# An MLP's first product on two row tiles: which output tiles share a two-bank PSUM buffer, and where the last eviction stands

## The chip, the cores and the metric

The kernel runs on one core of a Trainium2 chip. The metric is the device time of one execution in microseconds (us), as the median of several runs. The engines of the core run side by side, each through its own queue in order: TensorE (PE in the profile; its weight loads are PEld), VectorE (DVE), ScalarE (ACT), GpSimd (POOL) and SyncE (SP), which only issues transfers here. They wait for each other by semaphores.

## The reference

Four residual layers on a sequence of 2048 tokens with 576 features, in turn linear attention (A) and MLP (B), each applied to the layer-normalised input. The same weights serve both A layers and both B layers.

```python
B, S, D, F = 1, 2048, 576, 4608

def _B_ref(x, w1, b1, w2, b2):
    y = _layernorm(x, axis=-1)
    h = _gelu(jnp.einsum("bsd,df->bsf", y, w1) + b1)
    return jnp.einsum("bsf,fd->bsd", h, w2) + b2

x = x + _A_ref(_layernorm(x, axis=-1), A_wqkv, A_wo)
x = x + _B_ref(_layernorm(x, axis=-1), B_w1, B_b1, B_w2, B_b2)
x = x + _A_ref(_layernorm(x, axis=-1), A_wqkv, A_wo)
x = x + _B_ref(_layernorm(x, axis=-1), B_w1, B_b1, B_w2, B_b2)
```

The change is in the first product of the MLP, `y @ w1`, with its gelu.

## The kernel before

The tokens of an MLP layer are worked on in 4 chunks of 512. For one chunk the first product makes hT, the gelu of 4608 hidden features by 512 tokens, as 36 tiles of 128 x 512; `m1_group` makes four of them (n = 0 to 3), so a chunk has 9 groups, a layer 36, and the kernel 72. Then the second product (L546 to L560) makes four output tiles of 128 tokens from hT and w2, with accumulators of two PSUM banks, and adds the residual.

The contraction has 576 = 4 x 128 + 64 rows. [...] The odd 64 rows (`w1_tail`) go to the upper or the lower row tile by the parity of the tile. So each of the four tiles has nine matmuls, 4 or 5 from each row tile, and a group has 18 upper and 18 lower ones, interleaved one by one into 18 steps (numbered 0 to 17 here). The upper row tile takes the tiles in the order 0, 1, 2, 3, the lower one in the order 2, 3, 0, 1 (L501, L502):

| Steps | Upper row tile | Lower row tile |
|---|---|---|
| 0 to 3 | tile 0 | tile 2 |
| 4 | tile 0 | tile 3 |
| 5 to 8 | tile 1 | tile 3 |
| 9 to 12 | tile 2 | tile 0 |
| 13 | tile 2 | tile 1 |
| 14 to 17 | tile 3 | tile 1 |

Tile 0 is complete at step 12, tile 2 at step 13, tiles 3 and 1 at step 17. The order of TensorE's matmuls in the MLP is fixed by a chain of dependencies (`pe`).

Where a tile passes from one row tile to the other (from step 9 on), the matmul must not overlap the last one of the other row tile on the same bank. This is enforced over ScalarE: a tiny copy (L518, the relay) waits for the last matmul of the first holder, and the first matmul of the second holder waits for the relay. There are two relays in a group: one behind step 4 (tile 0's upper half; it lets tiles 0 and 2 change hands at step 9), one behind step 8 (tile 3's lower half; for tiles 1 and 3 at steps 13 and 14).

The four tiles lie in PSUM as follows: two buffers of one bank from the pool `ps_h`, which rotates over three, and a pair of banks from `ps_acc`, which has two such pairs used in turn (`next_acc`), the accumulators of the second product among them. Line 489 says which tile lies where: tiles 0 and 1 in the h buffers, tiles 2 and 3 in the pair. When a tile is complete, ScalarE evicts it with gelu and bias into hT (L524); ScalarE thus has the relays and the evictions in its queue. Dependencies between engines are found by the framework from the buffers that instructions read and write; a scheduler sets the order of each engine's instructions, as far as the chain and the dependencies leave it open.

The first two groups of a layer's first chunk are emitted in the tail of the attention layer before it (`a2_hook`, which calls `m1_group` after the last steps of that layer), so their matmuls can be placed between that layer's projections (`wo_ps`, L442), transposes (`to_ps`, L432) and numerators (`nd_ps`, L405). The buffer of hT overlays `abig`, the attention layer's buffer that the output projection reads.

Of the kernel before, what the change touches and what calls it, by code (L numbers as in the profile page):

```python
# [7 lines left out]
ACT = mybir.ActivationFunctionType  # L8
# [27 lines left out]
def build(tc, A_x, A_wqkv, A_wo, B_w1, B_b1, B_w2, B_b2, out, dbg=None, n_layers=4):  # L36
    nc = tc.nc
    dbg = dbg or {}
    with ExitStack() as ctx:
# [39 lines left out]
        b1T = const.tile([P, NF], F32, name="b1T")  # L79
# [30 lines left out]
        def pe(inst):  # L110
            if pe_chain["on"]:
                if pe_chain["last"] is not None:
                    tc.add_manual_dep(inst.ins, pe_chain["last"], NOSYNC, reason="TensorE order in the MLP")
                pe_chain["last"] = inst.ins.name
            return inst
# [10 lines left out]
        for t in range(5):  # L126
            load_x0(t)
        chained(nc.sync.dma_start(out=wqkv_sb[:, 0:4, D:3 * D],
                                  in_=A_wqkv[0:4 * P, D:3 * D].rearrange("(k p) n -> p k n", p=P)))
        chained(nc.sync.dma_start(out=wqkv_sb[0:64, 4, D:3 * D], in_=A_wqkv[4 * P:D, D:3 * D]))  # L130
        chained(nc.sync.dma_start(out=wqkv_sb[:, 0:4, 0:D],
                                  in_=A_wqkv[0:4 * P, 0:D].rearrange("(k p) n -> p k n", p=P)))
# [54 lines left out]
        class LNPipe:  # L187
            def __init__(self):
                self.items = []
# [86 lines left out]
        def prefetch_xo(li, t, add_b2):  # L276
            if li == 0:
                xo = work.tile([P, D], BF16, name="xbf", tag="xbf", bufs=5)
                nc.sync.dma_start(out=xo[:], in_=x_in[t * P:(t + 1) * P, :])
            else:  # L280
                xo = work.tile([P, D], F32, name="xo", tag="xo", bufs=3)
                nc.sync.dma_start(out=xo[:], in_=x_d[t])
            if add_b2:
                nc.gpsimd.tensor_tensor(out=xo[:], in0=xo[:], in1=b2_bc[:], op=ALU.add)  # L284
            xo_of[(li, t)] = xo

        def residual(li, t, halves):
            xo = xo_of.pop((li, t))
            last = (li == n_layers - 1)
            if last:  # L290
                xn = work.tile([P, D], BF16, name="xbf", tag="xbf", bufs=5)
            else:
                xn = work.tile([P, D], F32, name="xn", tag="xn", bufs=3)
            nc.vector.tensor_tensor(out=xn[:].rearrange("p (h n) -> p h n", h=2), in0=halves,  # L294
                                    in1=xo[:].rearrange("p (h n) -> p h n", h=2), op=ALU.add)
            if last:
                nc.sync.dma_start(out=out_f[t * P:(t + 1) * P, :], in_=xn[:])
                return None
            nc.sync.dma_start(out=x_d[t], in_=xn[:])
            return xn  # L300
# [165 lines left out]
        def next_acc():  # L466
            acc_turn["n"] += 1
            return ("accA", "accB")[acc_turn["n"] % 2]

        GF = 4  # L470
        NGRP = NF // GF

        class LayerB:
            def __init__(self, li, next_kind):
                self.li = li
                self.next_kind = next_kind
                self.hT = {}
                self.done = {}

            def m1_group(self, c, g):  # L480
                if c not in self.hT:
                    if c == 0:
                        acc_turn["n"] = 1
                    self.hT[c] = big.tile([P, NF, CB], BF16, name="hT", tag="big")
                hT = self.hT[c]
                ctok = slice(c * CB, (c + 1) * CB)
                hps = [ps_h.tile([P, 512], F32, name="h_ps", tag="h") for _ in range(2)]
                pair = ps_acc.tile([P, 2, 512], F32, name="hp_ps", tag=next_acc())
                dst = [hps[0][:], hps[1][:], pair[:, 0, :], pair[:, 1, :]]

                def half_blocks(n, hi):
                    f = g * GF + n
                    rows = slice(64 * hi, 64 * hi + 64)
                    ops = [(n, w1_sb[rows, k, f * P:(f + 1) * P], yT[rows, k, ctok]) for k in range(KD - 1)]
                    if f % 2 == hi:
                        fc = f // 2 * P
                        ops.append((n, w1_tail[rows, fc:fc + P], yT[rows, KD - 1, ctok]))
                    return ops

                was_on, pe_chain["on"] = pe_chain["on"], True  # L500
                upper = [op for n in (0, 1, 2, 3) for op in half_blocks(n, 0)]  # L501
                lower = [op for n in (2, 3, 0, 1) for op in half_blocks(n, 1)]  # L502
                seen = [0] * GF
                order = [(hi, n, wt, mv) for step in zip(upper, lower) for hi, (n, wt, mv) in enumerate(step)]
                first, last = {}, {}
                for i, (hi, n, _, _) in enumerate(order):
                    first.setdefault((hi, n), i)
                    last[(hi, n)] = i
                relay_at = {last[(0, 0)]: (0, 2), last[(1, 3)]: (1, 3)}
                starts = {first[(1, 0)]: 0, first[(0, 2)]: 2, first[(1, 1)]: 1, first[(0, 3)]: 3}  # L510
                relay_of = {}
                for i, (hi, n, wt, mv) in enumerate(order):
                    mm = pe(nc.tensor.matmul(dst[n], lhsT=wt, rhs=mv, start=(seen[n] == 0), stop=(seen[n] == 8)))  # L513
                    seen[n] += 1
                    if i in starts:
                        tc.add_manual_dep(mm.ins, relay_of[starts[i]], SYNC, reason="row tiles take turns on a PSUM bank")
                    if i in relay_at:
                        relay = nc.scalar.copy(out=relay_sb[:, 1:2], in_=relay_sb[:, 0:1])  # L518
                        tc.add_manual_dep(relay.ins, mm.ins.name, SYNC, reason="row tiles take turns on a PSUM bank")
                        for m in relay_at[i]:  # L520
                            relay_of[m] = relay.ins.name
                    if seen[n] == 9:
                        f = g * GF + n
                        nc.scalar.activation(out=hT[:, f, :], in_=dst[n], func=ACT.Gelu_apprx_tanh,  # L524
                                             bias=b1T[:, f:f + 1], scale=1.0)
                pe_chain["on"] = was_on
                self.done[c] = g + 1

            def run(self):
                li, next_kind = self.li, self.next_kind  # L530

                def feed_next(c, i):
                    if c + 1 < NCB:
                        t = (c + 1) * TPC + i
                        lnp.feed(None, t, "B", "dve", "dve", load_from=t)

                for c in range(NCB):
                    for g in range(self.done.get(c, 0), NGRP):
                        self.m1_group(c, g)
                        if g in (3, 5):  # L540
                            prefetch_xo(li, c * TPC + (g - 3) // 2, add_b2=True)
                        if g in (4, 6):
                            feed_next(c, (g - 4) // 2)
                        lnp.tick(transposes=0)
                    hT = self.hT.pop(c)
                    for j in range(TPC):  # L546
                        t = c * TPC + j
                        acc = ps_acc.tile([P, 2, 512], F32, name="m2_ps", tag=next_acc())
                        for f in range(NF):
                            for half in range(2):  # L550
                                pe(nc.tensor.matmul(acc[:, half, 0:HALF], lhsT=hT[:, f, j * P:(j + 1) * P],  # L551
                                                    rhs=w2_sb[:, f, half * HALF:(half + 1) * HALF],
                                                    start=(f == 0), stop=(f == NF - 1)))
                            if f % 12 == 6:
                                if j == 0 and f in (6, 18):
                                    feed_next(c, 2 + f // 18)
                                lnp.tick()
                            if f == 18 and j < 2:
                                prefetch_xo(li, c * TPC + 2 + j, add_b2=True)
                        xn = residual(li, t, acc[:, :, 0:HALF])  # L560
                        if xn is not None and next_kind == "A":
                            lnp.feed(xn, t, "A", "dve", "dve")
# [110 lines left out]
```

## Time and profile before

| | us |
|---|---|
| Median of 3 runs (lowest, highest) | 908.98 (908.51, 909.83) |
| The profiled execution's own time | 908.65 |
| Its span in the trace | 906.6 |
| TensorE busy | 801.6 (88%) |
| ScalarE busy | 356.9 (39%) |
| VectorE busy | 270.4 (30%) |
| GpSimd busy | 106.2 (12%) |
| First product, second chunk of layer 1 (window 214.6 to 261.5) | 46.9, TensorE busy 36.7 |
| Second product behind it (window 261.5 to 299.0) | 37.5, TensorE busy 37.5 |
| Granted TensorE clock from 117 us on | 1.00 (0.96 before) |

A line of the profile names the source line (L513 is line 513), the engine, the operation, the tile written, an arrow, the tiles read, and the shape. Tile names in it are the program's: `h_ps` and `hp_ps` are the h buffers and the pair of the first product, `m_ps` the accumulator of the second, `w_sb` any of the weights. Busy time of TensorE is modelled: its matmuls are pipelined, and the 376 ns that each matmul of L513 has in the profile overlap the next one. Idle time is put down to the instruction whose semaphore event came last before the wait ended. Matmuls and their weight loads are separate instructions; a wait can stand at either.

### The profile page before, as it was taken

What the parts mean: (1) busy time and instruction counts of PE and PEld (TensorE: products, weight loads), DVE (VectorE), ACT (ScalarE), POOL (GpSimd) and SP (SyncE); (2) the same over time, 40 slices, a digit from 0 to 9 for tenths busy, and PEclk for the clock granted to TensorE, in tenths of its full rate; (3) what the DMA queues carried; (4) which work ended last, traced back from release to release, by engine and by line L of the source; (5) the groups of instructions that cost most, each with busy time, mean ns of one, the idle gap of its engine ahead of it and who ended that gap; (6) DMA issues with size and microseconds to landing.
All of it is one profiled execution on the core that took longest, in us unless ns stands there. A gap on an engine that the chain in (4) does not pass through costs nothing.

```text
span 906.6 us, 16729 instructions
## 1 busy us (share of the span) xinstructions
PE 801.6 (88%) x7030; PEld 538.2 (59%) x7030; DVE 270.4 (30%) x850; ACT 356.9 (39%) x746; POOL 106.2 (12%) x199
## 2 busy tenths in 40 slices
PE   5999987798789879978999998879977987898798
PEld 3787654485358436734877776436734854584366
DVE  4757960035014402300244599202300300010001
ACT  4686735402530351055227674551055015303510
POOL 5410300012002201100100011201100210011000
PEclk8899999999999999999999999999999999999999
DMA  8970640012012100100110047201200210020000
GB/s 217 274 242 24 213 164 1 1 53 79 2 27 80 53 1 27 54 27 1 53 54 1 2 153 249 96 1 47 81 5 2 66 40 1 1 57 23 1 21 20
DMA packets 42907, 56.97 MB, mean 63 GB/s; under 512 B 10256, under 2 KB 26896, under 8 KB 42832
## 3 DMA queue, kind: packets, MB, share of 16 engines
q1 hardware_dynamic: 42832, 55.91, 20.3%
q8 instruction: 55, 0.90, 0.4%
q14 instruction: 20, 0.16, 0.1%
HBM read 39.38 MB, written 16.52 MB: 62 GB/s over the span
## 4 chain that ended last, share of the span: by engine, by line
PE 79%; ACT 11%; DVE 4%; issue 2%; DMA 1%; POOL 1%; DVEq 0%; POOLq 0%; ACTq 0%
PE m_ps L551 31%; PE h_ps L513 15%; PE hp_ps L513 15%; ACT hT L524 10%; PE q_ps L351 4%; PE k_ps L319 3%; PE v_ps L330 2%; PE wo_ps L442 2%; PE v_ps L327 2%; PE tp L250 2%; DVE xn L294 1%; PE kvacc L343 1%; PE to_ps L432 1%; DVE o_ring L416 1%; PE nd_ps L405 1%
## 5 line engine op out<-in xcount | busy, mean ns | idle before, releaser
L513 PE MATMUL hp_ps<-yT,w_sb 64*128 64x512 bf16 x1152 | 274.1, 376 | 81.4 <-ACT hT L524 81.4
L551 PE MATMUL m_ps<-w_sb,hT 128*128 128x288 bf16 x2304 | 289.8, 286 | 0.0
L513 PE MATMUL h_ps<-yT,w_sb 64*128 64x512 bf16 x1152 | 286.0, 377 | 0.0
L513 PEld LDWEIGHTS <-w_sb 64*128 64x128 bf16 x2304 | 137.5, 94 | 215.0 <-issue 104.5
L551 PEld LDWEIGHTS <-hT 128*128 128x128 bf16 x2304 | 223.2, 98 | 57.9 <-issue 3.4
L518 ACT COPY relay_sb<-relay_sb 128x1 f32<-128x1 f32 x144 | 27.4, 190 | 272.5 <-PE h_ps L513 224.0
L524 ACT ACTIVATE hT<-hp_ps,b1T 128x512 bf16<-128x512 f32 x144 | 98.4, 683 | 78.7 <-PE h_ps L513 78.7
L524 ACT ACTIVATE hT<-h_ps,b1T 128x512 bf16<-128x512 f32 x144 | 98.4, 683 | 45.0 <-PE h_ps L513 43.3
L254 DVE COPY yT<-tp 128x640 bf16<-128x640 bf16 x40 | 19.6, 490 | 323.5 <-PE tp L250 323.4
L225 POOL TENSOR_TENSOR ln_rstd<-ln_u,neg_half 128x1 f32<-128x1 f32 x64 | 36.0, 563 | 359.5 <-DVE ln_u L218 217.4
L284 POOL TENSOR_TENSOR xo<-xo,b_bc 128x576 f32<-128x576 f32 x32 | 40.8, 1276 | 177.4 <-DMA xo<-x_d 177.3
L513 PE MATMUL h_ps<-yT,w_tail 64*128 64x512 bf16 x144 | 54.1, 376 | 0.0
L513 PE MATMUL hp_ps<-yT,w_tail 64*128 64x512 bf16 x144 | 54.1, 376 | 0.0
L351 PE MATMUL q_ps<-yT,wqkv_sb 128*126 128x512 bf16 (+1 forms) x200 | 51.8, 381 | 0.0
L442 PE MATMUL wo_ps<-wo_sb,abig 128*128 128x288 bf16 x320 | 46.5, 286 | 5.0 <-ACT abig L434 3.4
L270 DVE TENSOR_SCALAR phi_e<-phi_e 128x288 bf16<-128x288 bf16 (+2 forms) x104 | 30.1, 290 | 60.9 <-ACT phi_e L267 60.4
L294 DVE TENSOR_TENSOR xbf<-m_ps,xo 128x576 bf16<-128x576 f32 x16 | 12.1, 758 | 119.2 <-PE m_ps L551 119.2
L319 PE MATMUL k_ps<-wqkv_sb,yT 128*128 128x288 bf16 x320 | 47.0, 294 | 0.0
L243 POOL COPY y_ring<-y_ring 128x64 bf16<-128x64 bf16 x64 | 15.4, 244 | 228.5 <-DVE y_ring L241 199.1
L267 ACT ACTIVATE phi_e<-k_ps 128x288 bf16<-128x288 f32 x64 | 26.8, 420 | 37.3 <-PE k_ps L319 33.9
L442 PEld LDWEIGHTS <-abig 128*128 128x128 bf16 x320 | 29.4, 98 | 15.8 <-ACT abig L434 6.0
L272 DVE TENSOR_TENSOR abig<-phi_a,phi_e 128x288 bf16<-128x288 bf16 (+2 forms) x104 | 36.1, 348 | 7.6 <-ACT phi_a L269 1.8
(78 smaller groups left out, 696.4 us busy)
## 6 DMA issues: line engine op xcount, KB each, us to landing
x_d<-xn SPq DMA_DIRECT2D x48, 288.0 KB, 2.2
xo<-x_d SPq DMA_DIRECT2D x48, 288.0 KB, 3.0
xl<-x_d SPq DMA_DIRECT2D x24, 288.0 KB, 3.0
w_sb<-in_B_w_dram SPq DMA_DIRECT2D x6, 864.0 KB, 11.1
xbf<-in_A_x_dram SPq DMA_DIRECT2D x32, 144.0 KB, 3.4
w_sb<-in_B_w_dram SPq DMA_DIRECT2D x9, 512.0 KB, 5.0
out_dram<-xbf SPq DMA_DIRECT2D x16, 144.0 KB, 1.7
wqkv_sb<-in_A_wqkv_dram SPq DMA_DIRECT2D x1, 1152.0 KB, 7.8
```

The lines of the kernel that those rows point to most:

```text
L225: nc.gpsimd.tensor_tensor(out=rstd[:], in0=it["u"][:], in1=neg_half[:], op=ALU.pow)
L267: nc.scalar.activation(out=e[0:rows, 0:n], in_=ps_ap, func=ACT.Exp)
L270: nc.vector.tensor_scalar(out=e[0:rows, 0:n], in0=e[0:rows, 0:n], scalar1=1.0, scalar2=1e-6, op0=ALU.min, op1=ALU.add)
L272: nc.vector.tensor_tensor(out=out_ap, in0=a[0:rows, 0:n], in1=e[0:rows, 0:n], op=ALU.max)
L284: nc.gpsimd.tensor_tensor(out=xo[:], in0=xo[:], in1=b2_bc[:], op=ALU.add)
L319: nc.tensor.matmul(kp[:, 0:HALF], lhsT=yT[:, k, tok], rhs=wqkv_sb[:, k, D + half * HALF: D + (half + 1) * HALF], start=(k == 0), stop=(k = ...
L351: nc.tensor.matmul(qp[0:GR[g], :], lhsT=wqkv_sb[:, k, GO[g]:GO[g] + GR[g]], rhs=yT[:, k, c * CA:(c + 1) * CA], start=(k == 0), stop=(k == ...
L442: nc.tensor.matmul(wp[:, half, 0:HALF], lhsT=oT[:, k, :], rhs=wo_sb[:, k, half * HALF:(half + 1) * HALF], start=(k == 0), stop=(k == KD - 1))
L513: mm = pe(nc.tensor.matmul(dst[n], lhsT=wt, rhs=mv, start=(seen[n] == 0), stop=(seen[n] == 8)))
L518: relay = nc.scalar.copy(out=relay_sb[:, 1:2], in_=relay_sb[:, 0:1])
L524: nc.scalar.activation(out=hT[:, f, :], in_=dst[n], func=ACT.Gelu_apprx_tanh, bias=b1T[:, f:f + 1], scale=1.0)
L551: pe(nc.tensor.matmul(acc[:, half, 0:HALF], lhsT=hT[:, f, j * P:(j + 1) * P], rhs=w2_sb[:, f, half * HALF:(half + 1) * HALF], start=(f == ...
```

## The change

Tiles 1 and 2 change places: tiles 0 and 2 lie in the h buffers now, tiles 1 and 3 in the pair. Tile 3's eviction is no longer emitted where the tile is complete, but held: it is emitted behind the next group's first relay, or, for a chunk's last group, ahead of the second product (`flush`). The matmuls, their order in the MLP, the number of relays and of evictions, and the buffers' sizes stay.

```diff
+                self.held = None
...
-                dst = [hps[0][:], hps[1][:], pair[:, 0, :], pair[:, 1, :]]
+                dst = [hps[0][:], pair[:, 0, :], hps[1][:], pair[:, 1, :]]
...
+                def evict(n):
+                    f = g * GF + n
+                    nc.scalar.activation(out=hT[:, f, :], in_=dst[n], func=ACT.Gelu_apprx_tanh,
+                                         bias=b1T[:, f:f + 1], scale=1.0)
+
                 for i, (hi, n, wt, mv) in enumerate(order):
...
                         for m in relay_at[i]:
                             relay_of[m] = relay.ins.name
-                    if seen[n] == 9:
-                        f = g * GF + n
-                        nc.scalar.activation(out=hT[:, f, :], in_=dst[n], func=ACT.Gelu_apprx_tanh,
-                                             bias=b1T[:, f:f + 1], scale=1.0)
+                        if i == last[(0, 0)]:
+                            self.flush()
+                    if seen[n] == 9 and n != 3:
+                        evict(n)
+                self.held = lambda: evict(3)
...
+            def flush(self):
+                if self.held is not None:
+                    self.held()
+                    self.held = None
...
                         lnp.tick(transposes=0)
+                    self.flush()
                     hT = self.hT.pop(c)
```

## The prediction

> **What bounds the kernel now.** I first read the page's chain of the work that ended last, for the engine to look at.
>
> ```profile
> PE 79%; ACT 11%; DVE 4%; issue 2%; DMA 1%; POOL 1%; DVEq 0%; POOLq 0%; ACTq 0%
> PE m_ps L551 31%; PE h_ps L513 15%; PE hp_ps L513 15%; ACT hT L524 10%; PE q_ps L351 4%; PE k_ps L319 3%; PE v_ps L330 2%; PE wo_ps L442 2%; PE v_ps L327 2%; PE tp L250 2%; DVE xn L294 1%; PE kvacc L343 1%; PE to_ps L432 1%; DVE o_ring L416 1%; PE nd_ps L405 1%
> ```
>
> TensorE sets the time, except that a tenth of the chain is the gelu eviction of L524. So I asked the view of waits who waits for that.
>
> ```profile
> ACT hT L524 <- PE h_ps L513: 122.0, 141, 1.1
> PE hp_ps L513 <- ACT hT L524: 81.4, 72, 1.4
> ```
>
> The columns are total us, times, and the longest. There are 2 MLP layers x 4 chunks x 9 groups = 72 groups, so TensorE waits once in each. The timeline of one group shows where (start, duration; in brackets the idle time and who ended it).
>
> ```profile
> 148.79 0.38 PE L513 MATMUL h_ps<-yT,w_sb 64*128 64x512 bf16 x1
> 148.99 0.38 PE L513 MATMUL hp_ps<-yT,w_tail 64*128 64x512 bf16 x1
> 149.20 0.69 ACT L524 ACTIVATE hT<-h_ps,b1T 128x512 bf16<-128x512 f32 x1 [0.62 <-PE h_ps L513]
> 149.79 0.68 ACT L524 ACTIVATE hT<-hp_ps,b1T 128x512 bf16<-128x512 f32 x1
> 150.52 0.37 PE L513 MATMUL hp_ps<-yT,w_sb 64*128 64x512 bf16 x1 [1.14 <-ACT hT L524]
> 151.38 0.38 PE L513 MATMUL h_ps<-yT,w_sb 64*128 64x512 bf16 x1
> 151.58 0.69 ACT L524 ACTIVATE hT<-hp_ps,b1T 128x512 bf16<-128x512 f32 x1 [1.11 <-PE h_ps L513]
> 152.16 0.68 ACT L524 ACTIVATE hT<-h_ps,b1T 128x512 bf16<-128x512 f32 x1
> 152.73 0.19 ACT L518 COPY relay_sb<-relay_sb 128x1 f32<-128x1 f32 x1
> 153.59 0.19 ACT L518 COPY relay_sb<-relay_sb 128x1 f32<-128x1 f32 x1 [0.67 <-PE hp_ps L513]
> 154.19 0.38 PE L513 MATMUL hp_ps<-yT,w_tail 64*128 64x512 bf16 x1
> 154.40 0.69 ACT L524 ACTIVATE hT<-h_ps,b1T 128x512 bf16<-128x512 f32 x1 [0.62 <-PE h_ps L513]
> ```
>
> A group has 18 steps (0 to 17), each one matmul of the upper and one of the lower row tile; the row at 148.79 is step 12 (tile 0's last), 148.99 step 13 (tile 2's last), 150.52 step 14 (tile 3's first upper), 151.38 step 0 of the next group. Step 14 writes one bank of the pair buffer, and starts 0.05 us after the eviction of tile 2, which reads the other bank (149.79 + 0.68 = 150.47): TensorE waits for a reader of the same buffer, not of the same data. Nothing else stops it: from 150.52 (step 14) to 154.19 (step 13 of the next group) 17 steps take 3.67 us, 0.216 each, so 18 need 3.89, and the group takes 154.40 - 149.20 = 5.20. The wait costs 1.31 a group (the row's 1.14 plus pipelining lost).
>
> **What the change removes.** Tiles 1 and 3, which end together at step 17, now share the pair; tiles 0 and 2 have an h buffer each. The write of step 14 then meets no pending reader. Of 72 groups, 70 wait like this one; the first group of each MLP layer is taken below. 70 x 1.31 = 92.0 us removed, if nothing takes its place.
>
> **What may take its place.** The h buffers rotate over three slots, two a group, so tile 2 of the next group needs the slot from which tile 0 was evicted. Set T at step 0 of the next group. Tile 0's last matmul (step 12, lower) starts at T - 6 x 0.216 + 0.02 = T - 1.28; its eviction starts 0.41 later (148.79 to 149.20) and lasts 0.69, and TensorE answers within 0.05: T - 0.13. The first lower matmul stands at T + 0.02: hidden by 0.15 us, cover thin enough to name. If it were gone, each 0.1 us of lateness costs 64 x 0.1 = 6.4 us (8 groups with a predecessor in each of 8 chunks).
>
> ScalarE's queue: evictions follow each other at 0.585 (149.20 to 149.79), a relay copy 0.57 behind an eviction (152.16 to 152.73). Tile 0 at T - 0.87, tile 2 at T - 0.28, tile 1 at T + 0.30, tile 3 at T + 0.89. The title says that the fourth eviction stands behind the next group's first relay copy. In the built program's order it does not: in the steady groups ScalarE has tiles 0, 2, 1, 3 and then both relay copies, as the scheduler puts what is ready first. So what is queued behind the held eviction is the relay copy, at T + 1.46 to 1.65, where it was 1.35 to 1.54 after step 0. Its reader is step 9, matmul at T + 1.94, weight load some 0.2 earlier: still in time, by about 0.1. The second relay waits for step 8 (T + 1.74 + 0.46 = T + 2.20, ends 2.39; needed at step 13, T + 2.82), and tile 0's next eviction is due at T + 3.02. Price of both places: I take 0; the far end, one more eviction pitch in the way, would be 0.585 - 0.15 = 0.43 us a group, 64 x 0.43 = 28 us. The held closure adds no instruction; the flush before the second product keeps tile 3's eviction ahead of its reader (f = 35, some 70 matmuls of L551 at 0.1225 = 8 us later): 0.
>
> ScalarE as the bound: 4 x 0.683 + 2 x 0.190 = 3.11 us busy a group against TensorE's 3.89; no. [...]
>
> **The two joints from attention to MLP.** There the first eviction waits for the last output projection, since the MLP's hT overlays the buffer that this reads:
>
> ```profile
> 131.47 1.28 ACT L524 ACT_TABLE_LOAD   x1
> 132.17 1.40 PE L442 MATMUL wo_ps<-wo_sb,abig 128*128 128x288 bf16 x10
> 133.61 0.69 ACT L524 ACTIVATE hT<-h_ps,b1T 128x512 bf16<-128x512 f32 x1 [0.86 <-PE wo_ps L442]
> 134.93 0.37 PE L513 MATMUL hp_ps<-yT,w_sb 64*128 64x512 bf16 x1 [1.35 <-ACT hT L524]
> ```
>
> Before, group 1 starts at 135.78, 2.21 after the projection's end at 133.57. In the changed order the table load also stands behind that end, and group 0 is complete ahead of it; group 1's first lower matmul waits for 0.04 + 1.28 + 0.69 + 0.05 = 2.06 us. Gain 2 x 0.17 = 0.3. [...] The four steps that group 0 no longer has behind the projection (4 x 0.216 = 0.86) must fit into TensorE's gaps ahead of it, where it waits 0.38 to 0.84 us at a time; and VectorE now normalises (L241, 0.57) ahead of a residual and an o_ring. Bounds: 0 to 2 x (0.86 + 0.76) = 3.2; I take 1.0, since the timeline from 117 to 129 us shows TensorE idle 0.38, 0.84, 0.84 and 0.77 us there, room for the 0.86 at least.
>
> **MLP to attention, layer 1 to 2.** Seven k_ps matmuls (1.03 us at 428.29) had been put into the last group's wait, with two table loads on idle ScalarE. Now they stand after the MLP: + 1.0 (0 to 1.03). The loads vanish from idle time: 0. SP and POOL: the transfers keep their order but for one xl load and one residual write; normalisation for the next chunk (about 6 us by its rows) has four groups, 15 us, before its transpose: 0.
>
> Sum, against the profiled execution's 908.65 us (span 906.6; the median of the runs is 0.33 higher): 908.65 - 92.0 - 0.3 + 1.0 + 1.0 = 818.4.
>
> **The rivals.** *ScalarE answers late* (0.18): one of the covers of 0.10 and 0.15 us does not hold, and a short wait stands at step 0 or 9. For it: the margins are less than one step. Against: each latency was read from the same instructions in the same neighbourhood. At 0.2 us, 64 x 0.2 = 13: 831; range 823 to 846, the far end above.
>
> *The wait stays* (0.02): step 14 would still wait, 908. Against it, the built order shows the wait on ScalarE moved from step 14 to the first lower matmul.
>
> *Two row tiles on neighbouring banks* (0.04), the slower side. In all 72 groups before, the upper and the lower matmul of nearly every step write one h buffer and one bank of the pair; now 16 of 18 steps write two h buffers or the two banks of one pair at once, and no row shows that. If such writes took turns, a step would last as two full-array matmuls of 512 columns do (q_ps, 1.97 us for nine, 0.219 each): 0.44. 72 x 16 x 0.22 = +253: 1072. It decides against the change once a step is longer by 1.31/18 = 0.073. Against it: steps stay at 0.216 whichever of three h slots meets either pair. Below nothing there is no room, a step being already one matmul's time. I take 0.
>
> **How the numbers follow.** The forecast has 0.76, its own range 815 to 823 (joints -0.3 to +3.2, attention 0 to 1.03, small slips in 92.0). To leave out no more than 2 in 10, the range goes into the first rival up to 832, and to 814 below. A measurement of this kernel can tell about 0.2% (1.8 us) from no change: faster 0.76 + 0.18 = 0.94, same 0.02, slower 0.04.
>
> **What would show it.** Right: TensorE's wait for ACT hT at L513 falls from 81.4 us to about 4 (two waits of 2 us); a group's first evictions 3.89 apart; the first product's part of a chunk 35 us where the windows now have 46.9; L551 unchanged. A wait in each group of 0.1 to 0.3 at the first h_ps matmul or a relay's wait at PEld shows the first rival; steps longer than 0.216 the third; a granted clock below the 1.00 that the windows show in both products would stretch every step alike.

## The result, and the profile after

| | before | after |
|---|---|---|
| Median of the compared runs, us | 908.75 (907.55 to 909.83, 4 runs) | 819.54 (817.33 to 821.47, 4 runs) |
| Ratio, with its 95% interval | | 0.9018 (0.8987 to 0.9049) |
| The profiled execution: own time / span, us | 908.65 / 906.6 | 821.47 / 819.8 |
| Mean granted TensorE clock in it | 0.994 | 0.990 |

The changed kernel is 89.2 us faster by the medians. The forecast was 818.4 us, with a range of 814 to 832. The lines have moved: in the kernel after, the first product's matmul is L520, its eviction L516, the relay L525 and the second product's matmul L565. Upper and lower name the row tiles of TensorE that work on rows 0 to 63 and on rows 64 to 127 of each block of 128; in the trace of before their matmuls run side by side, with starts at 148.77 and 148.79 us and 0.38 us each. The relays keep the two from writing to one bank at the same time in every run, so none shows what would follow without them. First the page's chain of the work that ended last, of the kernel after:

```profile
PE 90%; DVE 3%; ACT 2%; issue 1%; POOL 1%; DMA 0%; SPq 0%; POOLq 0%; ACTq 0%; DVEq 0%
```

ScalarE had 11% of the chain and has 2%; the gelu eviction, 10% before, is no longer in the page's list of the chain by line. The costliest groups of instructions show who ended TensorE's idle time at the first product (the last two columns are busy us with the mean ns of one, and the idle us just before them):

```profile
L520 PE MATMUL hp_ps<-yT,w_sb 64*128 64x512 bf16 x1152 | 173.3, 379 | 0.0
L520 PE MATMUL h_ps<-yT,w_sb 64*128 64x512 bf16 x1152 | 157.1, 379 | 3.6 <-ACT hT L516 3.6
```

The wait for ACT hT at the pair, 81.4 us in 72 pieces before, is 0.0. What is left are 3.6 us in two pieces at the h buffers. One steady group of the kernel after in the timeline (start, duration; weight loads left out):

```profile
149.89 0.68 ACT L516 ACTIVATE hT<-h_ps,b1T 128x512 bf16<-128x512 f32 x1
150.46 1.27 ACT L516 ACTIVATE hT<-hp_ps,b1T 128x512 bf16<-128x512 f32 x2
151.60 0.21 ACT L525 COPY relay_sb<-relay_sb 128x1 f32<-128x1 f32 x1
152.38 0.19 ACT L525 COPY relay_sb<-relay_sb 128x1 f32<-128x1 f32 x1 [0.58 <-PE hp_ps L520]
...
153.19 1.26 ACT L516 ACTIVATE hT<-h_ps,b1T 128x512 bf16<-128x512 f32 x2 [0.62 <-PE h_ps L520]
...
154.35 1.27 ACT L516 ACTIVATE hT<-hp_ps,b1T 128x512 bf16<-128x512 f32 x2
```

ScalarE takes tiles 0 and 2 (h buffers), tiles 1 and 3 (pair), then both relays. The pair's evictions of two groups start 154.35 - 150.46 = 3.89 us apart, where a group took 5.20. The window of the first product in the second chunk of layer 1 (window, us, then busy us of PE, PEld, DVE, ACT and POOL, granted clock, DMA share, GB/s) shows the same for the nine groups of a chunk: 35.07 us, TensorE busy throughout, where it was 46.9 before:

```profile
206.77:241.84 35.07, 35.07 (x326) 15.55 (x325) 8.95 (x29) 22.88 (x52) 4.83 (x9) 1.00 0.11 35
```

Now the joint from attention to MLP, in the timeline of the kernel after:

```profile
133.35 1.40 PE L442 MATMUL wo_ps<-wo_sb,abig 128*128 128x288 bf16 x10
...
134.82 1.28 ACT L516 ACT_TABLE_LOAD   x1 [3.06 <-PE wo_ps L442]
136.11 1.26 ACT L516 ACTIVATE hT<-h_ps,b1T 128x512 bf16<-128x512 f32 x2
136.85 1.02 PE L520 MATMUL h_ps<-yT,w_sb 64*128 64x512 bf16 x7 [1.79 <-ACT hT L516]
...
137.71 1.90 PE L520 MATMUL hp_ps<-yT,w_sb 64*128 64x512 bf16 x8
...
139.40 2.10 PE L520 MATMUL h_ps<-yT,w_sb 64*128 64x512 bf16 x8
```

Group 1 waits for the table load and the first eviction behind the last projection, as worked out. But eight matmuls that take 1.0 to 1.2 us elsewhere then take 1.90 and 2.10. The windows' column of the granted clock (the first of the last three) says why:

```profile
134.70:137.00 2.30, 0.51 (x4) 0.18 (x5) 0.76 (x1) 2.17 (x3) 0.00 (x0) 1.00 0.27 102
137.00:139.00 2.00, 2.00 (x16) 0.89 (x14) 0.00 (x0) 1.61 (x4) 0.00 (x0) 0.69 0.08 30
139.00:141.00 2.00, 2.00 (x12) 0.85 (x10) 0.00 (x0) 0.19 (x1) 0.00 (x0) 0.50 0.00 0
141.00:143.00 2.00, 2.00 (x20) 1.12 (x18) 0.00 (x0) 1.46 (x3) 0.00 (x0) 0.96 0.00 0
```

The clock is halved from about 137.8 to 141.2, and again from 533.7 to 537.1 behind the second joint. In each place about 1.7 us of work is lost; the kernel before had 1.00 there.

By stages, between the same events of both traces (a joint ends where step 0 of group 1 stands, taken 0.02 us ahead of its first lower matmul):

| Stage | before | after | difference |
|---|---|---|---|
| Start to the last numerators (`nd_ps`) ahead of the MLP's first matmul | 117.12 | 117.89 | +0.77 |
| Joint 1, to group 1's start | 18.66 | 18.94 | +0.28 |
| MLP, layer 1, from group 1 | 331.10 | 286.80 | -44.30 |
| Attention, layer 2 | 90.25 | 91.21 | +0.96 |
| Joint 2 | 18.66 | 18.36 | -0.30 |
| MLP, layer 3, from group 1 | 330.8 | 286.6 | -44.2 |
| Span | 906.6 | 819.8 | -86.8 |

### The profile page after: what moved, and what is told of

Read it like the earlier page. It is cut to its first block, busy times and chain, and to the rows that moved or that the text cites. A ratio compares the mean times of both kernels' runs of the same rounds, so it can differ in the third digit from the quotient of the medians.

```text
span 819.8 us, 16729 instructions
## 1 busy us (share of the span) xinstructions
PE 792.6 (97%) x7030; PEld 527.7 (64%) x7030; DVE 270.1 (33%) x850; ACT 346.2 (42%) x744; POOL 106.1 (13%) x199
## 4 chain that ended last, share of the span: by engine, by line
PE 90%; DVE 3%; ACT 2%; issue 1%; POOL 1%; DMA 0%; SPq 0%; POOLq 0%; ACTq 0%; DVEq 0%
PE m_ps L565 35%; PE h_ps L520 18%; PE hp_ps L520 16%; PE q_ps L351 5%; PE k_ps L319 4%; PE wo_ps L442 3%; PE v_ps L330 2%; PE v_ps L327 2%; PE tp L250 2%; PE kvacc L343 1%; PE to_ps L432 1%; PE nd_ps L405 1%; DVE xn L294 1%; DMA xl<-x_d 0%; ACT phi_e L267 0%
## 5 line engine op out<-in xcount | busy, mean ns | idle before, releaser
L565 PE MATMUL m_ps<-w_sb,hT 128*128 128x288 bf16 x2304 | 289.8, 286 | 0.0
L565 PEld LDWEIGHTS <-hT 128*128 128x128 bf16 x2304 | 223.2, 98 | 57.9 <-issue 3.4
L520 PEld LDWEIGHTS <-w_sb 64*128 64x128 bf16 x2304 | 128.7, 95 | 137.0 <-issue 10.4
L520 PE MATMUL hp_ps<-yT,w_sb 64*128 64x512 bf16 x1152 | 173.3, 379 | 0.0
L520 PE MATMUL h_ps<-yT,w_sb 64*128 64x512 bf16 x1152 | 157.1, 379 | 3.6 <-ACT hT L516 3.6
L525 ACT COPY relay_sb<-relay_sb 128x1 f32<-128x1 f32 x144 | 28.5, 198 | 268.0 <-PE h_ps L520 221.2
L516 ACT ACTIVATE hT<-h_ps,b1T 128x512 bf16<-128x512 f32 x144 | 91.0, 683 | 43.6 <-PE h_ps L520 43.5
L516 ACT ACTIVATE hT<-hp_ps,b1T 128x512 bf16<-128x512 f32 x144 | 91.1, 692 | 0.0
L520 PE MATMUL hp_ps<-yT,w_tail 64*128 64x512 bf16 x144 | 54.6, 380 | 0.0
L520 PE MATMUL h_ps<-yT,w_tail 64*128 64x512 bf16 x144 | 54.4, 378 | 0.0
L442 PE MATMUL wo_ps<-wo_sb,abig 128*128 128x288 bf16 x320 | 46.9, 286 | 4.2 <-DVE xn L294 3.5
L520 PEld LDWEIGHTS <-w_tail 64*128 64x128 bf16 x288 | 27.3, 95 | 16.7 <-issue 0.5
```

The costliest lines, as they stand in the source:

```text
L442: nc.tensor.matmul(wp[:, half, 0:HALF], lhsT=oT[:, k, :], rhs=wo_sb[:, k, half * HALF:(half + 1) * HALF], start=(k == 0), stop=(k == KD - 1))
```

## The experiments

My theory: a write to the pair waits for every pending reader of that two-bank buffer, and it takes the exchange of the tiles and the held eviction together to remove this. The rivals were that one of the two alone does it, that the fourth eviction's place against the relay matters, and that ScalarE has more room than the 0.15 us worked out. The diffs are against the kernel after. The numbers beside each ratio are 95% intervals against the kernel before on the same chip.

**The exchange alone.** Tiles 1 and 3 share the pair, but tile 3 is evicted where it is complete.

```diff
-                    if seen[n] == 9 and n != 3:
+                    if seen[n] == 9:
                         evict(n)
-                self.held = lambda: evict(3)
```

> The new layout, but each tile evicted where it is complete, tile 3 too. Theory (a matmul waits for any pending reader of the buffer it writes): tile 1's last matmul, the lower one of step 17, is emitted behind tile 3's eviction and writes the same pair, so it now waits for that eviction: queued behind tile 2's it ends some 2.3 us after tile 0's last matmul, where step 17 is due 1.08 after it, so 1.24 late in each group; the group takes 3.89 + 1.24 = 5.13 in place of 5.20, and the time is 900 to 908. Rival (the layout alone does it, the hold is decoration): 816 to 823.

Measured: 908.88 us (907.25 to 909.85, 8 runs), ratio 1.0000 (0.9987 to 1.0012). The wait has moved, as its timeline shows:

```profile
149.03 0.69 ACT L516 ACTIVATE hT<-hp_ps,b1T 128x512 bf16<-128x512 f32 x1
149.77 0.37 PE L520 MATMUL hp_ps<-yT,w_tail 64*128 64x512 bf16 x1 [1.05 <-ACT hT L516]
150.18 0.69 ACT L516 ACTIVATE hT<-hp_ps,b1T 128x512 bf16<-128x512 f32 x1 [0.46 <-PE hp_ps L520]
...
154.88 0.37 PE L520 MATMUL hp_ps<-yT,w_tail 64*128 64x512 bf16 x1 [1.05 <-ACT hT L516]
```

Step 17's lower matmul, tile 1's last (149.77), waits for tile 3's eviction (149.03 + 0.69 = 149.72), which reads the other bank of the pair; tile 1's own eviction follows at 150.18. So the layout alone only carries the wait from step 14 to step 17. A group takes 154.88 - 149.77 = 5.11 us, 0.09 less than before, so 70 x 0.09 = 6.3 us should have been gained; the kernel as a whole gained nothing, and the theory's expectation was missed by 0.9 us. The waits at the two joints grew from 1.35 to 3.26 us each (3.8 together), and behind the first one the granted clock was lowered for twice as long (0.50 from 135.8 to 142.6, 6.8 us):

```profile
135.00:137.00 2.00, 0.40 (x3) 0.69 0.37 141
137.00:139.00 2.00, 2.00 (x12) 0.50 0.00 0
139.00:141.00 2.00, 2.00 (x12) 0.50 0.00 0
141.00:143.00 2.00, 2.00 (x15) 0.60 0.00 0
```

(TensorE alone: window, us, its busy us, granted clock, DMA share, GB/s.)

**The hold alone.** The tiles lie as before; tile 3's eviction is held.

```diff
-                dst = [hps[0][:], pair[:, 0, :], hps[1][:], pair[:, 1, :]]
+                dst = [hps[0][:], hps[1][:], pair[:, 0, :], pair[:, 1, :]]
```

> The old layout, with tile 3's eviction held as in the change. Theory: step 14 still writes the pair that tile 2's eviction reads; the wait of 1.14 stays in each group, 906 to 911. Rival (the gain comes from what the held eviction leaves free in ScalarE's queue): 880 or less.

Measured: 909.24 us (907.19 to 911.25, 8 runs), ratio 1.0001 (0.9985 to 1.0018). In its view of waits (total us, times, longest) the old wait is complete:

```profile
PE hp_ps L520 <- ACT hT L516: 81.5, 72, 1.4
```

Neither part alone changes the time by more than the noise.

**No carrying past the group.** Tile 3's eviction is emitted at the end of its own group, behind tile 1's last matmul.

```diff
-                self.held = lambda: evict(3)
+                evict(3)
```

> The new layout, with tile 3's eviction emitted at the end of its own group, behind tile 1's, and nothing carried into the next group. Theory: the scheduler already puts the held eviction there, so this is the changed kernel again: 816 to 822, a group 3.89. Rival (carrying it past the group matters): 824 or more.

Measured: 817.78 us (815.86 to 820.57, 4 runs), ratio 0.9001 (0.8978 to 0.9024): the change's time. The held eviction only has to stand behind the last matmul that writes the pair; it could have been emitted right behind the group's loop.

**The order of the title, enforced.** An order-only dependency puts the fourth eviction on ScalarE really behind the next group's first relay.

```diff
+                    if behind is not None:
+                        tc.add_manual_dep(ev.ins, behind, NOSYNC, reason="fourth eviction behind the relay")
...
-                            self.flush()
+                            self.flush(relay.ins.name)
```

> As the change, with a scheduling dependency that really puts tile 3's eviction behind the next group's first relay copy, which the built order of the change does not. Theory: the relay then starts when step 4 is done, T + 1.32, the eviction runs T + 1.51 to 2.20, the second relay at T + 2.20 as before, tile 0's eviction at T + 3.02 as before: no difference from the change, 816 to 822. Rival (the eviction, kept back by the relay's wait for step 4, makes the second relay or tile 0's eviction late): 0.1 us or more a group, 824 or more.

Measured: 818.22 us (815.05 to 820.61, 4 runs), ratio 0.8992 (0.8969 to 0.9014). The timeline shows that the order is now the title's:

```profile
146.48 0.69 ACT L516 ACTIVATE hT<-hp_ps,b1T 128x512 bf16<-128x512 f32 x1
...
147.34 0.19 ACT L527 COPY relay_sb<-relay_sb 128x1 f32<-128x1 f32 x1 [0.17 <-PE h_ps L522]
147.44 0.68 ACT L516 ACTIVATE hT<-hp_ps,b1T 128x512 bf16<-128x512 f32 x1
```

The place against the relay costs and brings nothing that these runs can tell.

**The change again**, on the chip on which the next one and the two with the early table ran:

> The changed kernel again, beside the next two. Four runs of it stood at 817.3, 817.9, 821.1 and 821.5. Theory: two kinds of execution, near 817.5 and near 821.3, apart by one or two stretches of some 3.4 us behind the joints in which the granted clock is 0.50.

Measured: 819.77 us (818.76 to 821.73, 5 runs), ratio 0.9027 (0.9010 to 0.9043). In its profile the clock stayed at 1.00 behind the first joint and fell to 0.50 behind the second, after waits of 1.79 and 1.78 us. So behind pauses of one length the clock was lowered at one place and not at the other. The five runs do not form the two kinds that were expected: they lie between 818.76 and 821.73.

**More work on ScalarE.** Two gelu evictions of 128 x 512, whose results nobody uses, stand behind each group's second relay, except in the first two groups of a layer. This measures the cover at step 0.

```diff
+                        elif c > 0 or g >= 2:
+                            for pad in range(2):
+                                nc.scalar.activation(out=o_ring[pad][:, 0:512], in_=b2_bc[:, 0:512], func=ACT.Gelu_apprx_tanh,
+                                                     bias=relay_sb[:, 1:2], scale=1.0)
```

> As the change, with two more gelus of 128x512 on ScalarE behind the second relay of each group (all but the first two of a layer), into unused columns of a ring buffer; they only take time. Theory: the second relay ends at T + 2.39; the two take 2 x 0.585 behind it, so tile 0's eviction starts at 3.6 instead of 3.02, 0.6 late, of which 0.15 is covered; 60 groups have a successor that waits: 60 x 0.45 = +27, 840 to 852. Rival (the cover is larger than worked out): under 830. Rival (more than one place becomes late): over 855.

Measured: 848.79 us (847.46 to 849.87, 4 runs), ratio 0.9340 (0.9323 to 0.9357), 29.0 us above the change. Its timeline:

```profile
151.95 1.33 ACT L533 ACTIVATE o_ring<-b_bc,relay_sb 128x512 bf16<-128x512 bf16 x2
153.19 1.24 ACT L516 ACTIVATE hT<-h_ps,b1T 128x512 bf16<-128x512 f32 x2
153.91 1.02 PE L520 MATMUL h_ps<-yT,w_sb 64*128 64x512 bf16 x7 [0.23 <-ACT hT L516]
...
157.56 1.24 ACT L516 ACTIVATE hT<-h_ps,b1T 128x512 bf16<-128x512 f32 x2
```

The first h_ps matmul of the next group now waits, as the rival "ScalarE answers late" had it, and the group takes 157.56 - 153.19 = 4.37 us, 0.48 more than 3.89. There are 60 groups behind one with the extra work in the same chunk (6 + 3 x 8 in each of two layers); 60 x 0.48 = 28.8. The view of waits has that place (two of its 56 pieces, 1.8 us each, are at the joints), and a second one, where the weight load of step 9 waits for the relay:

```profile
PE h_ps L520 <- ACT hT L516: 16.2, 56, 1.8
PEld L520 <- ACT relay_sb L525: 12.8, 62, 0.2
```

In the kernel after, ScalarE sits idle from the second relay's end (152.38 + 0.19) to tile 0's eviction (153.19), 0.62 us. The two extra ones take 153.19 - 151.95 = 1.24, so tile 0's eviction is 0.62 late; less the cover of 0.15 that is 0.47, and 0.48 was measured.

**One eviction more** tests the same sum from the other side: 0.62 + 0.15 = 0.77 us of room should hold a single one.

```diff
-                            for pad in range(2):
+                            for pad in range(1):
```

(The diff is against the kernel with two.)

> One extra 128 x 512 gelu, whose result nobody uses, stands on ScalarE behind each group's second relay (not in the first two groups of a layer); otherwise the changed kernel. The two extra ones cost 0.48 us a group. In the changed kernel ScalarE sits idle for 0.62 us ahead of tile 0's eviction, and the cover worked out at step 0 is 0.15 us more, so there is room for about 0.77 us; one extra eviction takes 0.62. Theory: it is hidden, group 3.89 us, no wait of the first h_ps matmul in steady groups, time that of the changed kernel, 818 to 822 us. Rival (there is no room beyond what the two evictions showed, each costs half of their 0.48): group 4.13, 60 x 0.24 = 14 us more, 830 to 838. If the relay of step 9 is what is late: group 3.95 to 4.05, 824 to 830, with a wait for relay_sb at the weight loads.

Measured: 818.73 us (817.79 to 820.66, 4 runs), ratio 0.9009 (0.8990 to 0.9029). Its timeline:

```profile
151.24 0.72 ACT L533 ACTIVATE o_ring<-b_bc,relay_sb 128x512 bf16<-128x512 bf16 x1
151.87 1.25 ACT L516 ACTIVATE hT<-h_ps,b1T 128x512 bf16<-128x512 f32 x2
...
155.75 1.25 ACT L516 ACTIVATE hT<-h_ps,b1T 128x512 bf16<-128x512 f32 x2
```

The group is 155.75 - 151.87 = 3.88, and the extra eviction is hidden. Room ends between one and two. The single one takes up the 0.62 us of idle time and hardly needs the cover, so the 0.15 itself rests on the run with two.

**The table load off the joint.** The relays of a layer's first group are made a gelu of a zero, so that ScalarE loads gelu's table there, ahead of the last projection.

```diff
-                        relay = nc.scalar.copy(out=relay_sb[:, 1:2], in_=relay_sb[:, 0:1])
+                        if c == 0 and g == 0:
+                            relay = nc.scalar.activation(out=relay_sb[:, 1:2], in_=relay_sb[:, 0:1],
+                                                         func=ACT.Gelu_apprx_tanh)
+                        else:
+                            relay = nc.scalar.copy(out=relay_sb[:, 1:2], in_=relay_sb[:, 0:1])
```

> As the change, but the two relays of a layer's first group are gelus of a zero, so that the gelu table is loaded ahead of them, where ScalarE idles. Theory: TensorE's wait at the joint falls from 2.1 to 0.8 us, 2 x 1.28 = 2.6 us; and with less of a pause the clock no longer drops behind it: 814.5 to 815.5 in all runs. If the pause is not what makes the clock drop: 815 in some runs and 818.5 in others. Rival (the table load is hidden by other work at the joint): 817 to 821.

Measured: 815.41 us (813.78 to 818.02, 4 runs), ratio 0.8976 (0.8957 to 0.8996). The wait at the joint is shorter by the load's 1.28 us:

```profile
133.05 1.26 ACT L516 ACTIVATE hT<-h_ps,b1T 128x512 bf16<-128x512 f32 x2 [3.06 <-PE wo_ps L442]
133.79 1.02 PE L520 MATMUL h_ps<-yT,w_sb 64*128 64x512 bf16 x7 [0.51 <-ACT hT L516]
```

Two joints make 2 x 1.28 = 2.6; the medians differ by 4.4 from the change's. The rest, 1.8, has the size of one lost piece of clock (1.7 us), and the mean granted clock of the runs, 0.995 against 0.992, agrees. The time expected for all runs, 814.5 to 815.5, was missed: they lie between 813.78 and 818.02. The trace is of the fastest, so why one took 818.02, at a clock of 0.993, is open.

**And half a group kept back.** As above, and the second half of group 0 (steps 9 to 17) is emitted behind the last projection, so that TensorE has work while the first evictions run. (`m1_steps` is `m1_group` as a generator that stops ahead of step 9; this is the part of the diff that calls it.)

```diff
-                if s in (14, 15):
-                    lb.m1_group(0, s - 14)
+                if s == 14:
+                    lb.part = lb.m1_steps(0, 0, 18)
+                    next(lb.part)
+                elif s == 15:
+                    for _ in lb.part:
+                        pass
+                    lb.m1_group(0, 1)
```

> As e5_table_early, and group 0 of each layer is emitted in two parts, steps 0 to 8 and 9 to 17, with the last output projection between them. Theory: the projection is done before tile 0 is, so the first eviction waits for its own product alone, and group 1 starts with no wait: a further 0.7 us at each of two joints, 813 to 814.5, and no clock drop. Rival (the projection, moved ahead, waits for its own inputs and TensorE idles there): no gain over e5_table_early, or a loss of up to 1 us a joint.

Measured: 814.66 us (813.96 to 815.52, 4 runs), ratio 0.8966 (0.8951 to 0.8980), by the median 0.16 us above the expected 813 to 814.5. Its timeline at the first joint has no idle time of TensorE that an eviction ended (L528 and L520 are its matmul and eviction):

```profile
130.91 1.39 PE L442 MATMUL wo_ps<-wo_sb,abig 128*128 128x288 bf16 x10
132.23 1.04 PE L528 MATMUL h_ps<-yT,w_sb 64*128 64x512 bf16 x8
...
133.36 1.26 ACT L520 ACTIVATE hT<-h_ps,b1T 128x512 bf16<-128x512 f32 x2 [2.24 <-PE h_ps L528]
```

This is the best version found, 5.1 us below the change on the same chip (814.66 / 819.77 = 0.994; the two intervals against the kernel before do not meet). Against the version with the early table alone, 0.75 us, it can't be told apart. With the early table the pauses are short or gone, and neither profile shows a lowered clock behind a joint.

## Why the prediction was right

- **The wait and its removal.** Both place and size were right. (70 x 1.31 is 91.7; the 92.0 comes from 1.314, unrounded.) Of the two MLP stages' 44.3 and 44.2 us, the lowered clock took back 1.7 each; without it they are 46.0 and 45.9, together 91.9 where 92.0 was put. That the wait is for any pending reader of the two-bank buffer is shown by the two parts alone: each leaves a pending reader (tile 3's, or tile 2's), each in the other bank than the write, and each has the wait in every group (1.05 us with the exchange alone, 81.5 us in 72 pieces with the hold alone). By this reading a pair split into two one-bank buffers would lose the wait as well; that was not run.
- **Nothing takes its place.** This was right. The cover of 0.15 us at step 0 is confirmed by the two extra evictions, which cost 0.48 us a group where 0.47 follows from it; a single one stayed hidden. The rival "ScalarE answers late" did not come about. At step 9 the margin is thin as well: with two extra evictions the relay came up to 0.2 us late there.
- **Step 9 and the held eviction's place.** The built order does differ from the title's, as predicted, and the enforced order shows that it would not have mattered.
- **Two row tiles on neighbouring banks.** The rival is false: 3.89 us a group is 18 steps of 0.216, with two h buffers or both banks of a pair written at once.
- **The joints.** They were put at -0.3 + 1.0 and measured +0.28 - 0.30, so about 0 before the clock's loss. The wait was right: group 1's first lower matmul starts 136.85 - 134.75 = 2.10 us behind the projection's end, where 2.06 was worked out (TensorE's idle time there is 1.79, as one upper matmul of group 1 runs in between). What was put too high is the tail, 1.0 within bounds of 0 to 3.2: it cost about 0.2, so TensorE's gaps ahead of the projection held nearly all the displaced steps.
- **MLP to attention.** This was put at +1.0 and measured +0.96.
- **What was not priced.** The granted clock behind the joints, named among the things that would make the prediction wrong, but without a number: 2 x 1.7 = 3.4 us in the profiled execution. The start differed by +0.77 us; this need not be the change's doing, since the repetition of the changed kernel reaches the same place at 116.76 us, 1.13 earlier than its first profile (117.89). So the sum 818.4 against the profiled 821.47 is short by 3.4 (clock) + 0.8 (start) - 0.7 (joints) = 3.5, less 0.4 in what lies around the span (2.05 us before, 1.67 after), which is the 3.1 found. That the median of all runs came within 1.1 us of the forecast is in part luck: the tail, put 0.7 too high, made up for some of the clock, which was not in the sum.

## What to carry to other kernels

The two-bank PSUM buffer was one thing to the dependencies of the framework here: a tile that was complete early and evicted held up the writes to its neighbour bank, by 1.31 us a group. Put tiles that finish together into one buffer, and emit their evictions behind the last write to either; both were needed here, and neither alone changed the time measurably (ratios 1.0000 and 1.0001). When such a wait is gone, look at what is left at the stage joints: here the table load of 1.28 us on ScalarE moved ahead when a tiny earlier instruction was given the same function, and TensorE's wait fell from 1.79 to 0.51 us.

## What the runs showed of the hardware

**Behind pauses of 1.8 us the granted clock fell to 0.50 at 4 of 12 joints.** The granted TensorE clock fell to 0.50 for about 3.4 us behind the joints in some executions only: after 1.8 us of waiting, both joints in the change's profile, one of two in its repetition and in the enforced order, none in the version with the eviction at the group's end or in those with extra evictions, so at 4 of these 12 joints. After 3.26 us (exchange alone) it lasted twice as long, 6.8 us, at one joint and did not come at the other. After 1.35 us (before) and 0.51 us (early table) it was not seen. Each piece of 3.4 us cost 1.7 us. The change's first four runs spread over 4.1 us, of which 3.3 follow from their mean granted clocks (0.990 to 0.994 of 820 us). The start-up has pieces too: counting 1 minus the clock over windows of 1 us, 5.1 us are lost there in most profiles and 3.4 in others. With all of them taken off the spans, the profiles line up:

| Kernel | span | lost at the start | lost at the joints | span less both |
|---|---|---|---|---|
| before | 906.6 | 5.1 | 0 | 901.5 |
| exchange alone | 905.5 | 3.4 | 3.4 | 898.7 |
| hold alone | 907.9 | 5.1 | 0 | 902.8 |
| change | 819.8 | 5.1 | 3.4 | 811.3 |
| change again | 816.9 | 5.1 | 1.7 | 810.1 |
| eviction at the group's end | 814.1 | 3.4 | 0 | 810.7 |
| enforced order | 818.8 | 5.1 | 1.7 | 812.0 |
| one more eviction | 817.3 | 5.1 | 0 | 812.2 |
| two more evictions | 846.0 | 5.1 | 0 | 840.9 |
| early table | 812.1 | 3.4 | 0 | 808.7 |
| early table, half group | 812.2 | 5.1 | 0 | 807.1 |

This counts lost clock as lost time, which is an upper bound where TensorE waits anyway, at the start above all. On this footing the change is worth 90.2 to 91.4 us, where the sum had 90.3, and the exchange alone is worth 2.8 (its groups' 6.3 less 3.8 at the joints make 2.5): its small gain was there, and the clock covered it in this profile. Its eight runs say the same: their mean granted clock was 0.991, that of the 19 runs of the kernel before 0.995, which is some 3.5 us of 907.

Which joints lost clock goes, for the most part, with where the pause lay. In each of the eleven profiles all changes of the granted clock, at the start-up and behind the joints, were measured at whole multiples of 3.41 us from each other (in the change's profile at 11.46, 14.87, 21.70, 28.53, 137.75, 141.17, 533.70 and 537.11). This grid lay differently in each: the first change stood between 11.10 us (early table, half group) and 13.06 us (one more eviction). At the four joints with a lowered clock the pause of 1.8 us began 0.41 (enforced order), 0.72 and 1.17 (change) and 1.45 us (change again) behind a line of the grid and ended ahead of the next line, so TensorE was busy for 1.63 of these 3.41 us; the next 3.41 us then ran at 0.50. At the eight others, with 1.00 behind them, the pause ran across a line (five, beginning 1.70 us or more behind the one before) or began only 0.32 to 0.36 us behind a line (three). The two pauses of 3.26 us fit: the clock fell to 0.50 with the one that began 0.98 us behind a line, and not with the one that began at 1.60 and was cut by the next line into 1.81 and 1.45 us. No run moved the pause on purpose, so this is a pattern of 14 joints and not a test; why the clock stayed at 1.00 behind the three that began just behind a line is open. Whether the shorter pause of the early table (0.51 us) always avoids the loss is open too.
